# One block's forward transform by tokens mod 4, and wider VectorE instructions, in a fused convolution and feed-forward kernel

## The chip, the cores and the metric

The kernel runs on one core of one Trainium2 chip. A core has a matrix engine (TensorE, PE in the profile), a vector engine (VectorE, DVE), a scalar engine (ScalarE, ACT), a general engine (GpSimd, POOL) and a queue engine (SyncE, SP) that here mostly issues DMA transfers. The metric is the device time of one execution in microseconds (us); three runs of the kernel before took 908.04 to 908.59, median 908.13.

## The reference

Two layers of the same two steps, each added to its input: a gated long convolution (A) and a gated feed-forward network (B). S is 2048 tokens, D is 576, F is 4608. Cut to what matters:

```python
def A(q, k, v):                                # q is the normalised x
    kv = shift4(k, shift_k) * v                # four taps along the tokens
    y  = irfft(rfft(kv, 2*S) * rfft(ssm_k, 2*S))[:S]      # causal long convolution, per column
    return q * (y + kv * ssm_D)
def B(x):
    return (gelu(x @ w_gate) * (x @ w_up)) @ w_down
x = q
for layer in range(2):
    x = x + A(layernorm(x), k, v)
    x = x + B(layernorm(x))
```

## The kernel before, in words

**Blocks and units.** The 2048 tokens are four chunks (blocks) of 512. The convolution depends on neither layer's input, only on k, v and the filter, so its result y is made once for each block and used by both layers. A unit is one chunk of one layer; there are eight. The convolution is done blockwise in the frequency domain. Block m's product k\*v (`kvt`, from the tap products in L254 and L260) is turned into a spectrum `kc`, which has four row groups (`kt` 0 to 3) of 128 frequencies with two planes (`s`, real and imaginary, of 576 columns). The filter's block becomes a spectrum `hh`, later `hr`. VectorE multiplies spectra (`mul`, L337 for the real part as one instruction of 2 x 576 columns, L340 for the imaginary part as two of 576, since there the planes of the second factor are crossed), joins the two products (L343), adds over earlier blocks (L558), forms sums and differences of row groups (`both`, L363), shifts them against the block before (`shifted`, L368) and folds them (`fold`, L593 and L594). TensorE's inverse (L383) makes y of it. Spectra that later blocks need are written to DRAM (`Kd`, `Hd`) by GpSimd and read back as `kr` and `hr`.

**Two ways forward.** `fwd` with `fwd_eo` serves block 1's k\*v: for each pair of row groups, plane and column half, four matmul terms give an even and an odd part, and `cross` (L332) adds and subtracts them straight into `kc`. This is 8 calls of 8 matmuls. Here a pair of row groups of kc is ready after half of the calls. `fwd4` with `quarter` serves the filter and blocks 2 and 3: the tokens are taken mod 4, a call has two terms, `cross` writes partial sums in float32 (`ab`, `cd`), and `second` (L671) adds and subtracts these into all four row groups. This is 8 calls of 4 matmuls, and more VectorE work. In both, a matmul is split into two 64-row halves (`both_steps`, L309); between the two steps stands a placeholder on ScalarE or VectorE (`hold`, L1149) that frees the banks in order.

**Feed-forward.** Each of the eight units is visited three times, a third of the hidden columns each time: 24 phases. A phase has 12 gate/up tiles of 18 matmuls (`gu`, L1120, 216 in all, 64 rows, 512 columns), whose results ScalarE and VectorE turn into `hT` (L1714 to L1724), and then 192 matmuls of 64 rows and 288 columns (`dn`, L1793) whose sums VectorE adds into `x_c` (L1823 to L1831). Unit 0 is visited first; then come the others in pairs.

**Order.** A planner in the kernel writes the order of the instructions out by hand: it keeps a model of the time on TensorE, VectorE and ScalarE (`Pace`; the `C_` constants are its costs) and between two feed-forward tiles puts in convolution work that, by that model, is ready (`fill` with queues `V`, `U`, `Pq`, `aq`, `vq`). A prologue of the first 40 us, ordered by a list scheduler, does block 0's convolution, the filter's first spectra and the normalisation of unit 0.

**Rows.** A unit's normalised rows come in four groups of 128 tokens (`xn`, L1033) and must be turned to columns (`xnT`). `spread` (L1072) does it with two DMA transposes on SP's queue (L1075). `spreads` (L1105) gives a group instead to `turn_row` (L1128), which does it with nine TensorE transposes (L1136) and a copy, if by the planner's time it comes within 5 us (`SLOW`) of the end of the visit.

**Names that the change touches.** `prod`, `mul`, `join`, `both`, `shifted`, `fold`, `second`, `step`, the pools `kcp` (spectra) and `ybp` (sums of row groups), the prologue's products, and one call of `fill` at the start of a visit.

## Time and profile before

| what | value |
| --- | --- |
| median of three runs | 908.13 us |
| the profiled execution | 908.22 us, of which the span is 906.4 |
| TensorE busy in the span | 901.6 us |
| VectorE busy | 556.9 us |
| ScalarE busy | 365.6 us |
| GpSimd busy | 149.1 us |

The span runs from the first to the last instruction of the profiled execution; the time of that run holds 1.8 us more. A row of a group of instructions reads: line, engine, operation, output<-inputs, shape, count, then busy time, mean duration of one in ns, and idle time of the engine before them with what ended it. A row of the chain of waits reads: start, duration, engine, operation, line, count. It is the chain of work that ended last, followed back. "cps" is the convolution's PSUM bank, "ps" the prologue's, "gu" and "dn" those of the feed-forward network.

### The profile page before, as it was taken

The numbers are of one execution on the slowest core, as the hardware profiler recorded it, in microseconds if no ns is written. First come the engines' busy times: TensorE is split into PE (matmuls) and PEld (weight loads), VectorE is DVE, ScalarE is ACT, GpSimd is POOL, SyncE is SP. The second block draws the span as 40 slices with busy tenths as digits, with TensorE's granted clock in tenths as the row PEclk, the third lists the DMA queues.
The fourth block names the chain that finished last, engine by engine and source line by source line (L and its number), as shares of the span: only waits on it lengthen the run. The fifth ranks groups of instructions, "written<-read, shape, count | busy, mean of one in ns | idle before, by whom it ended". The sixth has DMA issues, their size and how long they took to land.

```text
span 906.4 us, 24221 instructions
## 1 busy us (share of the span) xinstructions
PE 901.6 (99%) x10445; PEld 597.4 (66%) x10445; DVE 556.9 (61%) x1127; ACT 365.6 (40%) x677; POOL 149.1 (16%) x311
## 2 busy tenths in 40 slices
PE   9999999999999999999999999999999999999998
PEld 7757656577576575775766756757757657667666
DVE  8899988744899946668899734453333334433332
ACT  7785346634534456455245233351121224321211
POOL 5543104220223012321022002220000002100000
PEclk9999999999999999999999999999999999999999
DMA  9999966976529303995943702852720821887640
GB/s 246 310 246 266 263 161 115 197 233 128 196 67 243 105 2 73 276 186 125 234 162 82 160 18 72 149 107 66 135 80 3 157 79 10 142 182 181 132 105 27
DMA packets 128414, 129.70 MB, mean 143 GB/s; under 512 B 43570, under 2 KB 120627, under 8 KB 128308
## 3 DMA queue, kind: packets, MB, share of 16 engines
q1 hardware_dynamic: 119282, 93.22, 48.4%
q0 software_dynamic: 8880, 34.36, 11.2%
q8 instruction: 81, 1.33, 0.6%
q10 hardware_dynamic: 146, 0.59, 0.2%
q14 instruction: 25, 0.20, 0.1%
HBM read 106.91 MB, written 11.80 MB: 131 GB/s over the span
## 4 chain that ended last, share of the span: by engine, by line
PE 96%; DVE 1%; ACT 1%; POOL 1%; issue 0%; ACTq 0%; DVEq 0%
PE gu L1120 61%; PE dn L1793 29%; PE cps L309 2%; PE ps L283 2%; PE ps L1364 0%; PE ps L1499 0%; PE ps L1120 0%; PE dn L1752 0%; PE dn L1761 0%; PE ps L1275 0%; POOL rstd L1583 0%; ACT junk L958 0%; PE ps L1335 0%; PE cps L383 0%; DVE x_c L1823 0%
## 5 line engine op out<-in xcount | busy, mean ns | idle before, releaser
L1120 PE MATMUL gu<-xnT,wgu 64*128 64x512 bf16 x5148 | 561.2, 376 | 0.2
L1120 PEld LDWEIGHTS <-wgu 64*128 64x128 bf16 x5220 | 292.2, 94 | 262.5 <-issue 1.5
L1793 PE MATMUL dn<-wd,hT 64*128 64x288 bf16 x4512 | 293.7, 283 | 0.0
L1793 PEld LDWEIGHTS <-hT 64*128 64x128 bf16 x4512 | 252.8, 94 | 27.6
L1724 DVE TENSOR_TENSOR hT<-ga,gu 128x512 bf16<-128x512 f32 x174 | 119.4, 686 | 170.8 <-ACT ga L1723 170.6
L1723 ACT ACTIVATE ga<-gu 128x512 f32<-128x512 f32 x174 | 103.8, 597 | 285.5 <-PE gu L1120 285.4
L1714 ACT ACTIVATE ga<-gu 128x512 bf16<-128x512 f32 x112 | 66.9, 597 | 138.3 <-PE gu L1120 133.6
L1716 DVE TENSOR_TENSOR hT<-ga 128x512 bf16<-128x512 bf16 x113 | 47.1, 420 | 51.1 <-ACT ga L1715 50.9
L1715 ACT CAST ga<-gu 128x512 bf16<-128x512 f32 x112 | 64.9, 579 | 0.0
L951 POOL TENSOR_SCALAR means<-s 128x1 f32<-128x1 f32 x28 | 18.4, 661 | 255.4 <-DVE x_c L1823 227.6
L1829 DVE SCALAR_TENSOR_TENSOR x_c<-dn,means,x_c 128x576 f32<-128x576 f32 x28 | 22.8, 815 | 29.6 <-PE dn L1793 29.6
L1831 DVE TENSOR_TENSOR x_c<-x_c,dn 128x576 f32<-128x576 f32 x32 | 24.0, 750 | 26.4 <-PE dn L1793 26.4
L327 ACT ACTIVATE eo<-cps 128x576 f32<-128x576 f32 x40 | 25.9, 651 | 27.5 <-PE cps L309 18.3
L966 POOL TENSOR_TENSOR rstd<-ve,neghalf_t 128x1 f32<-128x1 f32 x56 | 34.9, 624 | 4.7
L343 DVE TENSOR_TENSOR prod<-prod 128x576 bf16<-128x576 bf16 x64 | 29.0, 453 | 1.0
L1810 DVE TENSOR_TENSOR xn<-x_c,dn 128x576 bf16<-128x576 f32 x15 | 11.3, 753 | 25.5 <-PE dn L1793 23.2
L994 ACT ACTIVATE yh<-y,rstd 128x576 f32<-128x576 bf16 x28 | 21.4, 769 | 11.1 <-PE dn L1793 9.8
L671 DVE TENSOR_TENSOR kc<-ab,cd 128x288 bf16<-128x288 f32 x64 | 25.4, 449 | 0.0
L453 POOL DMA_DIRECT2D kr<-Kd x20 | 11.0, 549 | 86.9 <-DVE prod L337 86.9
L958 ACT ACTIVATE junk<-x_c,nm 128x576 bf16<-128x576 f32 x28 | 21.5, 768 | 2.0 <-POOL nm L951 1.6
L951 POOL TENSOR_SCALAR nm<-s 128x1 f32<-128x1 f32 x28 | 8.0, 286 | 79.1 <-DVE x_c L1004 79.0
L332 DVE TENSOR_TENSOR ab<-eo 128x288 f32<-128x288 f32 x40 | 16.1, 451 | 7.5 <-ACT eo L327 7.5
(179 smaller groups left out, 627.9 us busy)
## 6 DMA issues: line engine op xcount, KB each, us to landing
wgu<-in_B_w_gate_dram SPq DMA_DIRECT2D x45, 576.0 KB, 5.6
wd<-in_B_w_down_dram SPq DMA_DIRECT2D x30, 864.0 KB, 6.9
wgu<-in_B_w_up_dram SPq DMA_DIRECT2D x45, 512.0 KB, 7.6
hr<-Hd POOLq DMA_DIRECT2D x32, 288.0 KB, 5.6
kr<-Kd POOLq DMA_DIRECT2D x24, 288.0 KB, 5.5
Kd<-kc POOLq DMA_DIRECT2D x12, 288.0 KB, 6.5
k<-in_A_k_dram POOLq DMA_DIRECT2D x3, 1008.0 KB, 10.0
wgu<-in_B_w_up_dram SPq DMA_DIRECT2D x45, 64.0 KB, 7.2
```

Source lines behind the costliest of these rows:

```text
L327: nc.scalar.activation(out=eo[:], in_=ps[:, :, 0:HW], func=ACT.Copy, scale=scale)
L343: self.nc.vector.tensor_tensor(out=dst, in0=pr[:, 0, :], in1=pr[:, 1, :], op=ALU.subtract if part == 0 else ALU.add)
L671: nc.vector.tensor_tensor(out=into[k][:, plane, cols], in0=a, in1=b, op=op)
L951: nc.gpsimd.tensor_scalar(out=v["nm"][:], in0=v["s"][:], scalar1=-1.0 / D, scalar2=None, op0=ALU.mult)
L966: nc.gpsimd.tensor_tensor(out=v["rstd"][:], in0=ve[:], in1=neghalf_t[:, 0:1], op=ALU.pow)
L1120: nc.tensor.matmul(cols(pair[:, s, :]), lhsT=w[r0:r0 + HK, k, gi * P:(gi + 1) * P], rhs=cols(xnT[r0:r0 + HK, blk_of[k], :]), start=(k == 0 ...
L1714: nc.scalar.activation(out=ga[:, 0, :], in_=pair[:, 0, :], func=ACT.Gelu_apprx_tanh)
L1715: nc.scalar.copy(out=ga[:, 1, :], in_=pair[:, 1, :])
L1716: nc.vector.tensor_tensor(out=hT[:, fi, :], in0=ga[:, 0, :], in1=ga[:, 1, :], op=ALU.mult)
L1723: nc.scalar.activation(out=ga[:], in_=pair[:, 0, :], func=ACT.Gelu_apprx_tanh)
L1724: nc.vector.tensor_tensor(out=hT[:, fi, :], in0=ga[:], in1=pair[:, 1, :], op=ALU.mult)
L1793: nc.tensor.matmul(acc[:, g, 0:HW], lhsT=lhs[r], rhs=wn[r, g * HW:(g + 1) * HW], start=step == 0 and fi == 0, stop=step == 1 and fi == FP - 1)
```

## The change

1. Block 1's k\*v goes forward through `fwd4` like blocks 2 and 3; `fwd` and `fwd_eo` are gone. `kc` of a block is one tile of four row groups instead of four tiles, and is complete for all row groups at the same time. Its four row groups are written to `Kd` together.
2. The imaginary product is one instruction of 2 x 576 columns, which reads the second factor's planes in reverse order. `second` is one instruction of 2 x 288 columns for two row groups, `shifted` one of 2 x 576, and a fold takes two of 2 x 576 where it took four of 576, with reversed planes too. The tiles of `yb` are laid out to allow it (four tiles of 2 x 2 x 576 instead of sixteen of 576).
3. At the first visit, too, the planner may put convolution work (here two tap products) ahead of the first gate's `hT`, up to START = 2.1 us of its own time.
4. The constants of the planner's costs that went with the narrow instructions are dropped.

```diff
@@
-        self.kcp = pool("c_kc", N_KC)
-        self.ybp = pool("c_yb", 4 * RT)
+        self.kcp = pool("c_kc", 1)
+        self.ybp = pool("c_yb", RT)
@@ mul
-            for s in range(2):
-                nc.vector.tensor_tensor(out=pr[:, s, :], in0=K[:, s, :], in1=H[:, 1 - s, :], op=ALU.mult)
+            nc.vector.tensor_tensor(out=pr[:], in0=K[:], in1=H[:, ::-1, :], op=ALU.mult)
@@ shifted
-        self.nc.vector.tensor_tensor(out=prev[:], in0=now[:], in1=prev[:],
+        self.nc.vector.tensor_tensor(out=prev, in0=now, in1=prev,
                                      op=ALU.subtract if part == 0 else ALU.add)
@@ step, shift
-                for sg in range(2):
-                    prev = self.yb[(1 - part, kt, sg)]
-                    self.shifted(nyb[part, kt, sg], prev, part)
-                    z[(part, kt, sg)] = prev
+                prev = self.yb[kt][:, 1 - part, :, :]
+                self.shifted(nyb[kt][:, part, :, :], prev, part)
+                z[kt] = self.yb[kt]
@@ step, fold
-                    w["free"] = self.acp.tile([P, 2, D], BF16, tag="ac", name="w")[:, 0, :]
+                    w["free"] = self.acp.tile([P, 2, D], BF16, tag="ac", name="w")
+                    free = w["free"][:]
+                else:
+                    free = z[1][:, :, 0, :]
+                a, b = z[0][:, ::-1, sg, :], z[1][:, ::1 if sg else -1, sg, :]
+                self.nc.vector.tensor_tensor(out=free, in0=a, in1=b, op=ALU.add)
+                self.nc.vector.tensor_tensor(out=a, in0=a, in1=b, op=ALU.subtract)
                 for plane in range(2):
-                    a, b = z[plane, 0, sg][:], z[plane ^ sg, 1, sg][:]
                     up, down = (sg, sg + 2) if sg == 0 or plane else (sg + 2, sg)
-                    nc.vector.tensor_tensor(out=w["free"], in0=a, in1=b, op=ALU.add)
-                    nc.vector.tensor_tensor(out=a, in0=a, in1=b, op=ALU.subtract)
-                    w[up, plane], w[down, plane], w["free"] = w["free"], a, b
+                    w[up, plane], w[down, plane] = free[:, plane, :], z[0][:, 1 - plane, sg, :]
@@ step, second
-                        a, b = ab[s][:, n, :], ab["cd"][:, n, :]
-                        if n == 0:
-                            outs = ((0, s, ALU.add), (2, s, ALU.subtract))
-                        else:
-                            up = ALU.subtract if s == 0 else ALU.add
-                            outs = ((1, 1 - s, up), (3, 1 - s, ALU.add if s == 0 else ALU.subtract))
-                        for k, plane, op in outs:
-                            nc.vector.tensor_tensor(out=into[k][:, plane, cols], in0=a, in1=b, op=op)
-                        when = t.on_dve(2 * C_BF)
+                        rows = ((slice(0, 8, 7), slice(4, 2, -1)), (slice(1, 3, 1), slice(5, 7, 1)))[s][n]
+                        nc.vector.tensor_tensor(out=into["all"][:, rows, cols], in0=ab[s][:], in1=ab["cd"][:],
+                                                op=ALU.subtract if n else ALU.add)
+                        when = t.on_dve(C_M0)
@@ step, steps
-            if m > 1 or filt:
-                for h in range(2):
-                    for e in range(2):
-                        for s in range(2):
-                            self.Pq.append((limit, 0.25, fwd4(filt, e, s, h)))
-                return
-            for kt in range(2):
-                for s in range(2):
-                    for h in range(2):
-                        self.Pq.append((limit, 0.49, fwd(kt, s, h)))
+            for h in range(2):
+                for e in range(2):
+                    for s in range(2):
+                        self.Pq.append((limit, 0.25, fwd4(filt, e, s, h)))
@@ start of a visit
-            if at:
-                fill(t.pe + C_GU + 1.1, False, conv.left > 0)
+            fill(t.pe + (C_GU + 1.1 if at else START), False, conv.left > 0)
```

More of the change, by code (lines that the diff above doesn't have):

```diff
@@ L567, in run @@
             def run():
-                b = self.both(acc[kt - 2, part][:], acc[kt, part][:])
-                for sg in range(2):
-                    nyb[(part, kt - 2, sg)] = b[sg]
+                if kt - 2 not in nyb:
+                    self.plane_tiles(nyb, kt - 2)
+                self.both(acc[kt - 2, part][:], acc[kt, part][:], [nyb[part, kt - 2, sg] for sg in range(2)])
                 return lambda when: None
@@ L605, in step @@
         for kt in KTS:
-            ends = lambda part: [(now, 2 * C_EVD, both(kt, part)), (now, 2 * C_TB, shift(kt - 2, part))]
+            ends = lambda part: [(now, 2 * C_EVD, both(kt, part)), (now, C_M0, shift(kt - 2, part))]
             if m == 1:
@@ L626, in step @@
         for sg in range(2):
[L627 removed]
+            self.V.append((now, 2 * C_M0, fold(sg)))
         ab = {}
@@ L1470, in product @@
                     def product(m=m, part=part, h=h):
[L1471 to L1473 removed]
+                        if part == 0 and not h:
+                            t_ = conv.ybp.tile([P, 2, D], BF16, tag="yb", name="yb")
+                            for n in range(2):
+                                A[n, m] = t_[:, n, :]
+                        conv.prod(part, kc[m], h0[m], A[part, m], slice(0, D) if h is None else half[h])
                     pA[part, m, h or 0] = step = add("DVE", 1.2 if h is None else 0.75, product, (K0[m] if h is None else [K0[m][h]]) + H0[m])
```

99 lines of the change are left out of this document (28 added, 71 removed).

## The prediction

> **What bounds the kernel now.** I read the page's span and busy rows first, then the clock slices.
>
> ```profile
> span 906.4 us, 24221 instructions
> PE 901.6 (99%) x10445; PEld 597.4 (66%) x10445; DVE 556.9 (61%) x1127; ACT 365.6 (40%) x677; POOL 149.1 (16%) x311
> ```
>
> TensorE idles 4.8 us of 906.4. The busy times by stretch say where, and how close VectorE comes:
>
> ```profile
> core 0: us, PE busy (x) PEld busy (x) DVE busy (x) ACT busy (x) POOL busy (x), PEclk, DMA share, GB/s
> 0.00:40.10 40.10, 38.32 (x351) 30.22 (x353) 35.72 (x87) 29.74 (x50) 22.86 (x49) 1.00 1.01 282
> ...
> 44.56:64.78 20.22, 20.21 (x194) 11.02 (x195) 20.05 (x42) 16.15 (x34) 8.57 (x6) 1.00 0.98 245
> ...
> 80.55:104.87 24.32, 24.32 (x236) 13.08 (x234) 23.80 (x54) 12.92 (x25) 3.83 (x8) 1.00 0.97 317
> ...
> 142.20:155.81 13.61, 13.49 (x218) 10.85 (x215) 12.62 (x33) 8.43 (x17) 6.00 (x13) 1.00 0.52 89
> 155.81:868.41 712.60, 712.58 (x8330) 468.38 (x8331) 404.61 (x795) 260.20 (x486) 98.23 (x216) 1.00 0.56 129
> 868.41:906.40 37.99, 35.21 (x373) 22.43 (x368) 12.33 (x19) 7.17 (x12) 0.00 (x0) 1.00 0.13 40
> ```
>
> The granted clock is 1.00 throughout. TensorE loses 1.78 us in the prologue, 2.78 in the tail, 0.12 before 155.81, and 0.02 in the 712.6 us after that. So past 155.81 any TensorE work removed is time removed, and VectorE, busy 57% there, costs nothing. Before it VectorE is nearly as full as TensorE (20.05 of 20.22, 23.80 of 24.32), and block 1's whole chain on it must be ready by 155.81. The chain of waits shows that the two are level there:
>
> ```profile
> 104.87 11.76 PE dn L1793 x192
> 116.63 13.60 PE gu L1120 x126
> 130.23 1.09 PE cps L383 x8
> 131.31 2.05 PE gu L1120 x18
> ...
> 142.20 0.87 ACT junk L958 x2
> ...
> 154.28 0.81 DVE kc L671 x2
> 155.09 0.69 DVE x_c L1823 x2
> 155.81 23.49 PE gu L1120 x216
> ...
> 191.55 23.31 PE gu L1120 x216
> ```
>
> The release is the last of eight DMA transposes of unit 1's rows, which stand on SP's queue one behind another:
>
> ```profile
> L1075 SPq DMA_TRANSPOSE xnT<-xn x8: 1219/1254/2471, 142.9 to 153.3; - x8
> ...
> DMA to landing us min/median/max: 2.5/2.6/4.3
> ```
>
> The last starts at 153.3 and lands 2.6 us later, at 155.9: just where the next gate/up phase begins (155.81).
>
> **The change part by part.** *1. TensorE, block 1's k\*v.* Eight calls of eight 64-row matmuls (64) become eight of four (32). A 64-row matmul with 288 columns is half of a pair of the down projection's kind: 11.76 / 96 pairs = 0.1225 us (the row at 104.87: 192 matmuls). The 16 pairs removed are 16 x 0.1225 = 1.96 us. They stand amid full TensorE (24.32 busy of 24.32), so they come off the path.
>
> *2. TensorE, one row turned by nine transposes.* The reordering that I took from the two programs adds 18 TensorE rows: row 2 of unit 1's input, so far sent by DMA, goes through `turn_row` 112 matmuls into the phase ahead of 155.81. Its price is bounded by transposes that the trace has:
>
> ```profile
> 7.01 1.39 PE ps L1393 x20
> 9.97 0.45 PE ps L1320 x8
> 39.30 0.62 PE ps L1604 x8
> ```
>
> These are 0.070, 0.056 and 0.078 each, so nine cost 0.50 to 0.70. They run in 128-row form amid 64-row matmuls. What that costs shows around the inverse (above): eight 128-row matmuls take 1.09, against 8 x 0.1225 = 0.98, and the 18 gate/up matmuls behind them 2.05, against 23.31 / 12 = 1.94 (a phase of 216 without interruption, the row at 191.55), so 0.11 going in and 0.11 coming out. I take 0.50 + 0.22 = 0.72 (bounds 0.5 without any cost of the turn, 0.92 with both highest). TensorE's sum is -1.96 + 0.72 = -1.24 us.
>
> *3. VectorE, block 1.* The rows for what is merged and added:
>
> ```profile
> L254 DVE TENSOR_TENSOR kvt<-k,skc 128x1152 bf16<-128x1152 bf16 x24 | 17.9, 751 | 0.1
> L340 DVE TENSOR_TENSOR prod<-kr,hr 128x576 bf16<-128x576 bf16 x40 | 16.1, 449 | 0.0
> L337 DVE TENSOR_TENSOR prod<-kr,hr 128x1152 bf16<-128x1152 bf16 x20 | 14.8, 748 | 0.0
> ...
> 120.06 0.82 DVE L368 TENSOR_TENSOR yb<-yb 128x576 bf16<-128x576 bf16 x2
> 120.79 0.75 DVE L558 TENSOR_TENSOR ac<-hr,prod 128x576 f32<-128x576 bf16 x1
> ...
> 71.44 1.56 DVE L671 TENSOR_TENSOR hh<-ab,cd 128x288 bf16<-128x288 f32 x4
> ...
> 124.33 0.45 DVE L593 TENSOR_TENSOR w<-yb 128x576 bf16<-128x576 bf16 x1
> ...
> 127.98 0.46 DVE L594 TENSOR_TENSOR yb<-yb 128x576 bf16<-128x576 bf16 x1
> ```
>
> Two 576-wide operations issued together occupy about 0.74 (120.06 to 120.79); the 1152-wide one that replaces them shows 0.75 and lets the next start after 0.67. So a merge saves 0.07, a start-up and no throughput. Up to the folds block 1 has eight such products (-0.5) and four shifts (-0.3). The eight folds run from 124.33 to 128.44, 0.49 apart because each waits for the last; four wide ones at about 0.75 take 3.0 (-1.0). The filter's `second` step, four narrow operations in 1.47 (71.44 to 72.91), becomes two wide at 0.67 (-0.5 over its four). Two tap products of 0.67 move ahead of the first gate (-1.4). Against these, the new forward adds a `second` step: eight wide operations of 0.67 (+5.4), on a source in float32, for which L558's 0.75 at 576 wide is the nearest row. The sum is +5.4 - 0.5 - 0.3 - 1.0 - 0.5 - 1.4 = +1.7 us for VectorE ahead of block 1's inverse. In TensorE's order the inverse follows gate/up matmul 162 of the phase instead of 126: two tiles, 3.9 us, later, while the phase itself begins 1.96 earlier, at 114.67. So it would stand at 114.67 + 162 x 0.1079 = 132.15 instead of 130.23: 1.9 later on the clock, as much as its operands are, and it need not wait.
>
> *4. What follows the inverse.* With it the chain inverse, gate, norm and transposes shifts by 1.9 us, while TensorE arrives 1.24 earlier; in before the two met. Three things close this gap. Row 2 no longer stands on SP's queue (two transposes of 1.25 each, -2.5 on the queue). Six pairs of the next block's filter leave this phase for later ones, which takes 6 x 0.1225 = 0.74 from TensorE's side of the meeting (it is paid back later). Against it, SP issues that phase's third weight load ahead of the transposes, so they stand behind its issue; I put that at nothing, since it comes while the norms are still under way, and under (c) price what it could cost. I laid the operations of the new order end to end with the durations above. The inverse's second half ends at 136.4, the gates' and squares' chain gives xn rows at 144.8, 146.2, 147.7 and 149.15, TensorE reaches the nine transposes at 147.2 and waits 0.3 for row 2, and row 3's two DMA transposes land at 153.1 to 155.2. The two-step products with row halves wait for placeholder instructions on ScalarE, which in the new order stand behind squares:
>
> ```profile
> 149.83 0.77 ACT L958 ACTIVATE junk<-x_c,means 128x576 bf16<-128x576 f32 x1
> ```
>
> TensorE would stand behind such a square three times, 0.2 to 0.25 each. Unit 1 then begins at about 154.7 (153.7 to 155.6) instead of 155.81. That is -1.1, plus the 0.74 that comes later: -0.4. So of TensorE's -1.24 about 0.9 us goes into new waits.
>
> *5. Parts at nothing.* The two products ahead of the first gate fill an idle stretch:
>
> ```profile
> 43.82 0.69 DVE L1724 TENSOR_TENSOR hT<-ga,ps 128x512 bf16<-128x512 f32 x1 [2.59 <-ACT ga L1723]
> ```
>
> 1.34 into 2.59; if the kernel's first product slipped instead, at most 0.7 would be lost. The prologue's wide products run beside TensorE's 38.32 of 40.10; its last waits are for sums and roots on ScalarE and GpSimd, not for them (0 to 0.2 either way). The wider operations of blocks 2 and 3 lie under 712.58 of 712.60 TensorE time, VectorE at 57%: nothing. One y copy moves from ScalarE to VectorE; both have room there. Block 1's four `Kd` rows are written together and later on GpSimd's queue; their reader, block 2, works past 155.81, where no wait shows, so 0 (a wait there would appear in that stretch).
>
> Sum: 906.4 - 1.24 + 0.9 = 906.06, rounded 906.1. The profiled execution took 908.22, 1.8 more than its span, and stands 0.09 over the median of 908.13. So the forecast is 906.06 + 1.82 - 0.09 = 907.8 us.
>
> **The rivals.**
>
> *(a) TensorE's sum alone.* The chain keeps up, and no new wait appears: -1.24 and the 0.12 before 155.81, so 906.8. For it: 0.02 us of waits in 712 us show that the planner's order can hide everything. Against it: level chains at 155.81. 0.20.
>
> *(b) The reversed views run VectorE at half rate.* The wide products, and the folds, read one operand with its two halves in reverse order, which no row shows. If that drops it to one element a cycle, the price comes from the float32 rows: 576 wide takes 0.75 against 0.45 in bf16, so 0.3 per 576 and 0.6 per 1152. Twelve such operations ahead of block 1's inverse make +7.2 us; VectorE is otherwise full (23.80 of 24.32), and what idles there (the row below) could hide 58.43 - 56.35 = 2.1. TensorE waits at the inverse and again at 155.81 for about 5 us: 907.8 + 5.1 = 912.9. It decides from the point where the slowdown exceeds some 0.2 us an operation (2.4 in all). For it: float32 operands do lose rate. Against it: the inner run of 576 stays contiguous, and L337's 1152 in two rows runs at full rate. 0.10.
>
> ```profile
> 69.97:128.40 58.43, 58.43 (x708) 39.52 (x705) 56.35 (x125) 23.89 (x45) 9.23 (x17) 1.00 0.94 250
> ```
>
> [...]
>
> *(c) Block 1's chain is later than I laid it.* kc is now complete only after all eight quarters, where before each half freed its own products, and VectorE does 1.7 us more. If the products stall on that, or the third weight load, now ahead of the transposes on SP, holds them by one load's issue, then unit 1 begins at 156.5 to 158.5, not 154.7: 1.8 to 3.8 more, 909.6 to 911.6. Against it: the filter's and block 0's products are there to fill the gap. 0.13.
>
> *(d) The extra turn or its waits cost nothing at this place, while the moved pairs hide in waits:* 906.0 to 906.4. 0.07.
>
> **How the numbers follow.** My forecast has 0.50, with a range of its own of 907.1 to 908.7 (start of unit 1 at 153.7 to 155.6, turn 0.5 to 0.92). The predicted time is 907.8 us. For 8 in 10, the range takes in (a) whole and (d)'s top below, and the lower part of (c) above: 906.3 to 910.0. Below 0.2% (1.8 us, about what a measurement of this kernel tells from no change), that is, under 906.3, lies half of (d) and the edge of (a) and of the bounds: faster 0.11. Above 909.9 lie (b), most of (c) and a little of the bounds of the forecast: slower 0.20. Same: 0.69.
>
> **What would show it.** TensorE's instructions fall by 23 pairs of rows; the L309 group on v and nT is gone; nine transposes from L1136 stand once near 147. In the phase that begins near 114.7, the inverse (L383) starts near 132.2, without idle ahead of it. Unit 1's first gate/up matmul starts near 154.7, with 0.5 to 1.2 us of idle between 142 and there, and after it TensorE is again full. The wide part-1 products show about 0.75; 1.35 means (b). If TensorE waits at the inverse, or unit 1 begins after 155.8, the chain was laid too short; if the idle before unit 1 is under 0.2, (a) was right.

## The result, and the profile after

The changed kernel takes 909.48 us (median of 20 runs, 909.37 to 910.70), the kernel before 908.19 in runs interleaved with them (20 runs, 908.01 to 908.59). The ratio is 1.0015, with a 95% interval of 1.0009 to 1.0022: 1.3 us slower, where 0.3 us faster was forecast. Its first profile is that of its slowest run (910.70). The run `again`, of the same kernel, took 909.38, near the median, and its profile is used here. First its page: span and busy times.

```profile
span 907.6 us, 24074 instructions
PE 900.9 (99%) x10422; PEld 572.6 (63%) x10422; DVE 558.2 (62%) x1032; ACT 366.4 (40%) x678; POOL 144.1 (16%) x311
```

TensorE does 0.7 us less than before (900.9 against 901.6) and idles 1.9 more (907.6 - 900.9 = 6.7, against 4.8). The work came down and waits ate it. The busy times by stretch (columns as in the prediction) say where they are:

```profile
64.78:80.55 15.77, 15.58 (x246) 13.62 (x243) 13.41 (x26) 10.17 (x20) 8.10 (x15) 1.00 1.15 201
80.55:104.87 24.32, 24.32 (x244) 13.69 (x242) 23.11 (x48) 13.44 (x25) 4.82 (x9) 1.00 0.98 273
...
142.20:155.81 13.61, 12.29 (x195) 9.75 (x191) 11.42 (x29) 8.22 (x18) 8.76 (x19) 1.00 0.95 155
155.81:868.41 712.60, 712.06 (x8324) 445.23 (x8322) 406.94 (x732) 261.59 (x488) 96.44 (x214) 1.00 0.55 128
868.41:907.60 39.19, 36.29 (x390) 21.61 (x386) 12.74 (x20) 7.16 (x12) 0.00 (x0) 0.99 0.13 40
```

Most of it is ahead of unit 1: between 142.20 and 155.81 TensorE idles 1.32 us where it idled 0.12. After 155.81 it idles 0.54 where it idled 0.02, around 80 it idles 0.19, and the tail costs 2.90 instead of 2.78. The view of TensorE's waits between 40 and 910 us names them (us in total, times, the longest):

```profile
PE cps L298 <- ACT eo L316: 1.5, 3, 1.1
PE cps L1086 <- DVE xn L983: 0.2, 1, 0.2
PE gu L1070 <- DVE x_c L1780: 0.2, 1, 0.2
```

In the kernel before this view is empty (its 0.12 us ahead of unit 1 has no releaser there). Where the time is gained and lost shows in the starts of the phases. They come from the chain of waits of the changed kernel; the row at 155.53 is TensorE's own timeline, as the chain counts a phase's first matmuls to the one before.

```profile
103.19 11.76 PE dn L1744 x192
114.94 17.48 PE gu L1070 x162
132.43 1.09 PE cps L365 x8
133.51 2.05 PE gu L1070 x18
...
147.71 0.68 PE cps L1086 x9
...
191.88 23.31 PE gu L1070 x216
...
229.54 23.31 PE gu L1070 x216
...
411.62 23.31 PE gu L1070 x216
```

```profile
153.21 0.30 PE L298 MATMUL cps<-ht,T 64*128 64x288 bf16 x2 [1.09 <-ACT eo L316]
...
155.53 2.12 PE L1070 MATMUL gu<-xnT,wgu 64*128 64x512 bf16 x18
```

| start of | before | after | difference |
| --- | --- | --- | --- |
| unit 0's second `dn` phase | 104.87 | 103.19 | -1.68 |
| the gate/up phase with the inverse | 116.63 | 114.94 | -1.69 |
| the inverse | 130.23 | 132.43 | +2.20 |
| unit 1's first gate/up (TensorE's timeline) | 155.81 | 155.53 | -0.28 |
| the next visit | 191.55 | 191.88 | +0.33 |
| the phase after it | 228.73 | 229.54 | +0.81 |
| the phase at 411 | 410.54 | 411.62 | +1.08 |
| end of the span | 906.4 | 907.6 | +1.2 |

Read downwards: 1.68 us are gained by 103; 1.41 of them are gone when unit 1 begins (0.68 for the turn and 1.34 of waits and what else the turn costs, less the 0.61 of the pairs that left); five pairs of filter matmuls that left this phase (TensorE's timeline shows 7 from 139 us on where there were 12) are paid in the next (5 x 0.1225 = 0.61, which is the step from -0.28 to +0.33); and 0.5 more goes in each of two later phases of blocks 2 and 3, of which 0.2 comes back between them.

### The profile page after: what moved, and what is told of

It is laid out like the page before. It is cut to its first block, busy times and chain, and to the rows that moved or that the text cites. A ratio compares the mean times of both kernels' runs of the same rounds, so it can differ in the third digit from the quotient of the medians.

```text
span 908.9 us, 24074 instructions
## 1 busy us (share of the span) xinstructions
PE 901.1 (99%) x10422; PEld 576.0 (63%) x10422; DVE 558.3 (61%) x1032; ACT 366.6 (40%) x678; POOL 143.9 (16%) x311
## 4 chain that ended last, share of the span: by engine, by line
PE 94%; DVE 2%; DMA 1%; ACT 1%; issue 1%; POOL 1%; SPq 0%; ACTq 0%; DVEq 0%
PE gu L1070 61%; PE dn L1744 28%; PE ps L282 2%; PE cps L298 1%; DMA hn<-in_A_ssm_k_dram 1%; DVE kc L625 0%; DVE cd L321 0%; DMA xnT<-xn 0%; PE ps L1314 0%; DVE x_c L1780 0%; PE ps L1451 0%; PE ps L1070 0%; PE dn L1703 0%; PE dn L1712 0%; PE cps L365 0%
## 5 line engine op out<-in xcount | busy, mean ns | idle before, releaser
L1070 PEld LDWEIGHTS <-wgu 64*128 64x128 bf16 x5220 | 282.0, 94 | 273.6 <-issue 2.4
L1744 PEld LDWEIGHTS <-hT 64*128 64x128 bf16 x4512 | 242.8, 94 | 37.6
L901 POOL TENSOR_SCALAR means<-s 128x1 f32<-128x1 f32 x28 | 10.7, 384 | 262.8 <-DVE x_c L1774 224.5
L316 ACT ACTIVATE eo<-cps 128x576 f32<-128x576 f32 x48 | 30.9, 651 | 28.4 <-PE cps L298 21.5
L625 DVE TENSOR_TENSOR kc<-ab,cd 128x576 bf16<-128x576 f32 x40 | 29.2, 753 | 0.5
L321 DVE TENSOR_TENSOR ab<-eo 128x288 f32<-128x288 f32 x48 | 19.4, 453 | 7.5 <-ACT eo L316 7.5
L915 POOL TENSOR_SCALAR ve<-ss 128x1 f32<-128x1 f32 x56 | 16.5, 295 | 45.2 <-ACT junk L908 44.3
```

The source lines that it names most:

```text
L316: nc.scalar.activation(out=eo[:], in_=ps[:, :, 0:HW], func=ACT.Copy, scale=scale)
L625: nc.vector.tensor_tensor(out=into["all"][:, rows, cols], in0=ab[s][:], in1=ab["cd"][:], op=ALU.subtract if n else ALU.add)
L1070: nc.tensor.matmul(cols(pair[:, s, :]), lhsT=w[r0:r0 + HK, k, gi * P:(gi + 1) * P], rhs=cols(xnT[r0:r0 + HK, blk_of[k], :]), start=(k == 0 ...
L1744: nc.tensor.matmul(acc[:, g, 0:HW], lhsT=lhs[r], rhs=wn[r, g * HW:(g + 1) * HW], start=step == 0 and fi == 0, stop=step == 1 and fi == FP - 1)
```

## The experiments

Each was first a guess at the 1.4 us ahead of unit 1 or at the 0.5 behind it. The guesses were, in the order in which they came up: the weight load that now stands ahead of the transposes on SP; ScalarE's order, which holds TensorE 1.09 us at 153.21; three chains that end together, so that taking one away only shows the next; the wide instructions themselves; the planner's smaller costs, which change the order; and block 1's chain as a whole. "Before" below is always the kernel before, measured beside that version: 908.11 to 908.19.

### The same kernel again, and the weight load

`again` is the changed kernel unaltered. `load_late` holds the third weight load back until unit 1's transposes are issued; nothing else in any engine's order changes.

> The changed kernel once more, for its spread and a second profile. Its twenty runs so far fell into groups near 909.4, 909.8 and 910.7, and the profiled one (span 908.9) belongs to the slowest. Theory A (the weight load that now stands ahead of unit 1's DMA transposes on SP's queue makes them late): the groups differ by how the load's packets and the transposes' meet, so a profile of a run near 909.4 (span 907.6) shows TensorE's wait for the last transpose at 157.07 (0.91 us) gone or small, and the rest of the trace the same. Theory B (the loss lies in TensorE's wait for ScalarE, 1.09 us at 152.35, behind a gate): that wait is the one that changes, and the wait for the transposes stays near 0.9.

> The changed kernel with the third weight load of that phase put behind unit 1's transposes on SP's queue, as before; no other engine's order changes. Theory A: the transposes land in 2.6 us instead of 4.2, the last by about 153.5, TensorE starts unit 1 when its own work is done, near 155.8 instead of 157.07, and the time falls by 0.3 to 1.3, to 908.2 to 909.1. Theory B: TensorE arrives at 155.8 whatever the transposes do, ScalarE's wait decides, and the median changes by less than 0.2 (909.3 to 909.6).

```diff
-            if due[0][0] > t.pe + (HOLD if near else SOON):
+            if due[0][0] > t.pe + (HOLD if near else SOON) or due[0][2:] == (load_wgu, 11) and xn_done.get(1, 0) < RT:
                 break
```

`again` took 909.38 (909.36 to 909.76, 11 runs), `load_late` 909.39 (909.36 to 909.41, 11 runs). So the load is not the cause of the loss. It is seen in the slowest run's profile. Here are SP's timeline in that profile (910.70) and the transposes' own rows there, with the time to landing (minimum, median, maximum):

```profile
140.90 0.59 SPq L843 DMA_DIRECT2D wgu<-in_B_w_gate_dram  x1
...
145.29 9.52 SPq L1025 DMA_TRANSPOSE xnT<-xn  x6
```

```profile
L1025 SPq DMA_TRANSPOSE xnT<-xn x6: 1199/1242/2289, 145.3 to 153.3; - x6
...
DMA to landing us min/median/max: 2.6/4.2/5.4
```

and TensorE waits there once more than at the median:

```profile
PE gu L1070 <- DMA xnT<-xn: 0.9, 1, 0.9
```

In `load_late` the landing is back at 2.6:

```profile
L1025 SPq DMA_TRANSPOSE xnT<-xn x6: 1231/1242/2712, 145.1 to 153.1; - x6
...
DMA to landing us min/median/max: 2.5/2.6/4.6
```

The transposes land later while the load is under way (median 4.2 in the slow run, 3.6 in `again`); in `again` TensorE waits for none of them. With the load behind them 11 runs lie within 0.05 us. So in this order the spread comes with the load; the 1.3 us does not. (Later versions, in other orders, spread over 0.3 us and more with the load held back too.) The versions below hold the load back too, except `old_forward`, `cut_after` and `wide_old_plan`.

### The old forward transform, and no turn

`old_forward` gives block 1 the old forward transform back (`fwd` and `fwd_eo` as before) and keeps all else. `late_no_turn` sends row 2 by DMA again (`SLOW` 5.0 to 0.0).

> The changed kernel with block 1's k*v forward as before (eight calls of eight matmuls), everything else as changed. The planner puts its weight load behind the transposes and all eight transposes on SP's queue again, so this is before with wide VectorE instructions and the two early tap products. If the wide instructions cost nothing and the loss comes with the new forward through what the planner makes of it: 907.9 to 908.4, level with before. If the wide instructions themselves cost time (a wait of 0.1 for both inputs of each in the later forwards, reversed planes): 908.7 or more.

> As load_late, and row 2 of unit 1 is again turned by DMA (no nine transposes on TensorE, eight transposes on SP). Theory A with the price of the turn as predicted (0.7 on TensorE): TensorE gains 0.7, but the last transposes are issued 2.5 later and land near 155.9, level with TensorE; the time is 0.2 to 0.7 below load_late. If the transposes on one queue are what bounds unit 1's start even without the load: level with load_late or above it by up to 0.5.

`old_forward` took 912.02 (910.46 to 914.19, 5 runs): slower than either kernel. The profile is that of its fastest run; what the others lose beyond it was not profiled. TensorE's longest waits there are for VectorE's `hT`, and unit 1 begins at 157.78, with no wait just ahead of it:

```profile
PE dn L1785 <- DVE hT L1708: 0.5, 1, 0.5
...
PE gu L1111 <- DVE hT L1716: 0.4, 1, 0.4
```

Undoing one part let the planner make another order, so this run does not price the forward transform alone. That the order makes it slow, and not the old forward transform or the wide instructions, is shown by `wide_old_plan`, further down, which has both.

`late_no_turn` took 916.82 (915.90 to 917.25, 4 runs):

```profile
PE gu L1070 <- DVE kvt L253: 3.6, 1, 3.6
PE gu L1070 <- DMA xnT<-xn: 3.1, 1, 3.1
```

Eight transposes in a row were issued until 155.2 and landed by 160.5; besides, the new order puts four tap products ahead of an eviction. The 3.1 us for DMA alone is more than the turn's 0.68. Behind these waits TensorE also ran slower for a while: its granted clock was 0.50 from 158 to 162 us and 0.67 from 162 to 164, and the 214 gate/up matmuls from 160.53 took 24.63 us, 1.54 over 214 x 0.1079. So part of what this version loses is the clock. The turn costs time on TensorE and is worth more than it costs; it is not where the change loses.

### ScalarE's order ahead of unit 1

TensorE's 1.09 us at 153.21 ends with ScalarE's `eo`. ScalarE's timeline (`again`) shows what stood in front of it:

```profile
150.90 0.63 ACT L316 ACTIVATE eo<-cps 128x576 f32<-128x576 f32 x1
151.84 0.78 ACT L944 ACTIVATE yh<-y,rstd 128x576 f32<-128x576 bf16 x1 [0.32 <-POOL rstd L916]
152.53 0.63 ACT L316 ACTIVATE eo<-cps 128x576 f32<-128x576 f32 x1
```

The next unit's `yh` was put ahead of `eo`, and its `rstd`, made on GpSimd, came 0.32 late. `eo_first` makes the planner count that `rstd` 1.5 us later for this unit, so that `eo` goes first. `eo_turn3` does that and turns row 3 on TensorE too.

```diff
-            return max(conv.y_at.get((c, j), NEVER), g.get("rstd_at", NEVER))
+            return max(conv.y_at.get((c, j), NEVER), g.get("rstd_at", NEVER) + (1.5 if g["ui"] == units.index((1, 0)) else 0.0))
...
         while xn_made and (now or xn_made[0][3] <= t.pe):
+            if xn_made[0][0] == 1 and xn_made[0][1] == 3: break
```

> load_late, and in the stretch 149 to 158 ScalarE evicts the filter's spectrum (eo) before the gates of layer 1 instead of behind them, because the planner now counts these gates' roots as 1.5 us later; TensorE's and SP's orders are unchanged, VectorE's changes by a few neighbours. It takes away TensorE's wait of 1.09 us at 152.1. Theory B (that wait is the loss): TensorE reaches unit 1 at 154.5 instead of 155.5, and the time falls by 0.7 to 1.1, to 908.3 to 908.7. Theory C (two chains end together at 155.5: TensorE with its wait, and behind the same late inverse the last transpose, issued at 153.1 and landing 2.5 later): the wait at 152.1 is gone and one of about 1.0 for the transposes takes its place; the time stays within 0.2, 909.2 to 909.6.

> eo_first, and row 3 of unit 1 is also turned by nine TensorE transposes; SP has four DMA transposes left, the last landing near 151.6. Theory C: with both chains out of the way, TensorE pays 0.7 for the second turn and gains the 1.1, so the time falls by 0.2 to 0.6 against eo_first, to 908.8 to 909.3. Theory B: eo_first has the gain already, and this one loses the turn's price against it, +0.6 to 0.9.

`eo_first` took 909.78 (908.65 to 910.45, 11 runs), no better in the median and spread over 1.8 us. The wait for `eo` is gone, and TensorE waits for the transposes instead:

```profile
154.59 0.40 PE L1070 MATMUL gu<-xnT,wgu 64*128 64x512 bf16 x2
155.29 1.90 PE L1070 MATMUL gu<-xnT,wgu 64*128 64x512 bf16 x16 [0.30 <-DMA xnT<-xn]
```

Of the 0.94 us gained ahead of unit 1 (154.59 for 155.53) 0.48 is lost two matmuls later (155.29 - 154.59 - 2 x 0.1079). The profiled run took 909.02, under its median; what the others lose was not profiled. `eo_turn3` takes the transposes away too: 909.41 (909.29 to 909.85). Unit 1 then begins where the prediction had it:

```profile
154.75 3.83 PE L1071 MATMUL gu<-xnT,wgu 64*128 64x512 bf16 x33
```

But the next visit starts at 191.50, behind a wait for VectorE's eviction, only 0.2 ahead of `again` (191.71 in the same view), and the median is where it was:

```profile
191.50 1.26 PE L1071 MATMUL gu<-xnT,wgu 64*128 64x512 bf16 x10 [0.29 <-DVE x_c L1781]
```

Of the 0.78 us gained at unit 1, 0.29 is this wait and 0.12 a pair of filter matmuls that now comes later. So ScalarE's hold was not the only cause. Behind it stand the DMA transposes; with both out of the way unit 1 starts earlier, at the price of a second turn, and VectorE takes part of it at the next visit.

### The wide instructions

`narrow_second` and `narrow_rest` keep the order and issue the wide instructions as the narrow ones they replaced: the first `second` alone, the second products, shifts and folds.

```diff
-            nc.vector.tensor_tensor(out=pr[:], in0=K[:], in1=H[:, ::-1, :], op=ALU.mult)
+            for s in range(2): nc.vector.tensor_tensor(out=pr[:, s, :], in0=K[:, s, :], in1=H[:, 1 - s, :], op=ALU.mult)
...
-        self.nc.vector.tensor_tensor(out=prev, in0=now, in1=prev,
+        for i in range(2): self.nc.vector.tensor_tensor(out=prev[:, i, :], in0=now[:, i, :], in1=prev[:, i, :],
```

> load_late with the planner's order kept, but each wide instruction of `second` issued as two of 288 columns, first the sums and differences that need only the first of the two `cross` results, as before. Twice 0.37 for one 0.67, so +0.07 each on VectorE; in return the first need not wait for the second `cross` result (0.1). In the forwards of blocks 2 and 3 TensorE waits 0.2 for ScalarE's eviction behind VectorE, at 227 and at 409. If the wide form's longer dependence makes these waits: they shrink, and the time falls by 0.2 to 0.5. If they come from the planner's smaller cost for it (0.67 for 0.74), which puts the work closer together: the waits stay or grow, within 0.2 or up to 0.3 more.

> load_late with the planner's order kept, but the imaginary products, the shifts and the folds issued as narrow instructions as before (no reversed view is left but in `second`). Up to the folds that is 0.6 for the products, 0.3 for the shifts and up to 1.0 for the folds more on VectorE. Rival (b) of the prediction, reversed views at half rate: the time falls clearly, by 2 us or more. Otherwise the folds end 1 to 2 us later, TensorE waits for them at the inverse (its slack there is some 0.8), and the time rises by 0.2 to 1.2.

They took 909.47 (909.45 to 909.81) and 909.72 (909.69 to 909.99): the wide forms are worth 0.1 and 0.3 us, not a loss. The groups by line and shape of `again` show their rate; L326 is the forward view, L328 and L553 read reversed planes:

```profile
L625 DVE TENSOR_TENSOR kc<-ab,cd 128x576 bf16<-128x576 f32 x40 | 29.2, 753 | 0.5
L326 DVE TENSOR_TENSOR prod<-kr,hr 128x1152 bf16<-128x1152 bf16 x20 | 14.8, 751 | 0.0
L328 DVE TENSOR_TENSOR prod<-kr,hr 128x1152 bf16<-128x1152 bf16 x20 | 14.7, 752 | 0.0
...
L553 DVE TENSOR_TENSOR yb<-yb 128x1152 bf16<-128x1152 bf16 x6 | 4.5, 758 | 0.2
```

752 against 751 ns: the reversed view costs nothing.

### The planner's cost of `second`

The 0.5 us lost between 191.88 and 229.54 come with waits. This is TensorE's timeline of `again` there, and ScalarE's:

```profile
224.08 1.65 PE L1744 MATMUL dn<-wd,hT 64*128 64x288 bf16 x24
225.94 0.30 PE L298 MATMUL cps<-v,T 64*128 64x288 bf16 x2 [0.21 <-ACT eo L316]
...
226.67 1.41 PE L1744 MATMUL dn<-wd,hT 64*128 64x288 bf16 x20
228.14 0.30 PE L298 MATMUL cps<-v,T 64*128 64x288 bf16 x2
```

```profile
225.24 0.65 ACT L316 ACTIVATE eo<-cps 128x576 f32<-128x576 f32 x1 [1.46 <-DVE cd L321]
```

The kernel before has 28 and 24 down matmuls in the two gaps where this one has 24 and 20:

```profile
223.75 1.90 PE L1793 MATMUL dn<-wd,hT 64*128 64x288 bf16 x28
...
226.35 1.65 PE L1793 MATMUL dn<-wd,hT 64*128 64x288 bf16 x24
```

From the start of these matmuls to that of the next pair both kernels take the same time (1.87 and 1.47 us there, 1.86 and 1.47 here). So the eight matmuls (8 x 0.0613 = 0.49) are what this phase loses; of this only 0.21 shows as a wait in the timeline. The planner now counts a `second` at 0.67 instead of 0.74, believes VectorE free earlier and calls the next pair of block 2's forward transform (`v`) four matmuls (0.25 us) too soon; the pair waits for `eo`, which waits for VectorE. `second_cost` gives `second` its old planning cost for blocks 2 and 3 and changes no instruction.

```diff
-                        when = t.on_dve(C_M0)
+                        when = t.on_dve(C_M0 if m == 1 else 2 * C_BF)
...
-                    self.U.append((done + LAG, C_M0, second(0)))
-                    self.U.append((done + LAG, C_M0, second(1)))
+                    self.U.append((done + LAG, C_M0 if m == 1 else 2 * C_BF, second(0)))
+                    self.U.append((done + LAG, C_M0 if m == 1 else 2 * C_BF, second(1)))
```

> load_late, with the planner's cost of `second` in the forwards of blocks 2 and 3 put back from 0.67 to 0.74 an instruction; the instructions are the same. The planner then leaves 28 and 24 down-projection matmuls between the quarters there, as before, for 24 and 20, and the third block's inverse goes back to two phases. If the smaller cost made TensorE's waits at 226 and 408 (0.21 each, and what lies around them): both waits vanish, and the time falls by 0.4 to 1.0, to 908.4 to 909.0. If they come from VectorE's wide form or from something else: the waits stay, within 0.2 of 909.39.

It took 909.06 (908.80 to 909.49, 11 runs; ratio to before 1.0010, 1.0001 to 1.0019), 0.33 under `load_late`, a little less than the least that was expected (0.4). Its TensorE timeline at the same place:

```profile
224.08 1.90 PE L1744 MATMUL dn<-wd,hT 64*128 64x288 bf16 x28
225.93 0.30 PE L298 MATMUL cps<-v,T 64*128 64x288 bf16 x2
...
226.67 1.65 PE L1744 MATMUL dn<-wd,hT 64*128 64x288 bf16 x24
228.14 0.30 PE L298 MATMUL cps<-v,T 64*128 64x288 bf16 x2
```

The pairs start at the same times as in `again` (225.93 and 228.14), with eight more down matmuls done between them. The next phase starts at 229.05 instead of 229.54, the one at 411 at 410.65 instead of 411.62. Half of this 0.97 is lost again by 518, where a new wait of 0.33 stands, in block 3's inverse. Against the expectation, that inverse stays in one phase, as in the changed kernel; the kernel before has it in two.

```profile
510.80 0.42 PE L298 MATMUL cps<-yb,V 64*128 64x288 bf16 x4 [0.33 <-DVE x_c L1782]
```

### `second` on GpSimd

To take block 1's extra work off VectorE, `pool_early` issues block 1's eight `second` steps on GpSimd and lets the folds come 1 us earlier in the plan; `pool_early_cost` adds `second_cost`.

```diff
-                        nc.vector.tensor_tensor(out=into["all"][:, rows, cols], in0=ab[s][:], in1=ab["cd"][:],
+                        (nc.vector if m > 1 or filt else nc.gpsimd).tensor_tensor(out=into["all"][:, rows, cols], in0=ab[s][:], in1=ab["cd"][:],
...
-                        mark(("z", sg, part), when + LAG)
+                        mark(("z", sg, part), when + LAG - (1.0 if m == 1 else 0.0))
```

> load_late, with block 1's eight `second` instructions on GpSimd instead of VectorE (the planner counts nothing for them on VectorE and takes the folds as ready 1.0 earlier). The inverse goes one gate/up tile earlier, to matmul 144, and the planner turns all four rows by DMA. Theory D (block 1's work on VectorE, 5.4 us of it `second`, sets when the inverse and with it the rows and transposes of unit 1 come, and so takes what TensorE gains): the inverse starts near 130.5, the last transpose lands near 154, TensorE starts unit 1 near 153.5 to 154.5, and the time falls by 0.7 to 2.0, to 907.4 to 908.7. Rival E (the meeting at unit 1 is set by other things, ScalarE's and GpSimd's chains behind the inverse, or GpSimd is too slow for `second`): no fall, or a rise, 909.2 and more.

> Both edits. If the two causes are separate, their differences from load_late add up to within 0.3. With theory D and the first reading of second_cost: 906.6 to 908.1, below the kernel before.

They took 916.88 (916.36 to 919.57, 4 runs) and 917.07 (916.82 to 919.12, 4 runs). One such step takes GpSimd twice VectorE's time (median 1563 ns, where VectorE's `second` on the filter took 754 in this run; the row has minimum, median, maximum), and TensorE stands 5.4 us:

```profile
L625 POOL TENSOR_TENSOR kc<-ab,cd x8: 1391/1563/1917, 76.4 to 98.2; 128x576 bf16<-128x576 f32 x8
```

```profile
PE gu L1070 <- DVE x_c L1780: 5.4, 1, 5.4
```

Three things add up here. VectorE's next partial sums need the buffer that GpSimd still reads (two of them wait 2.7 and 2.6 us for it), and the eviction stands behind them. Behind this wait the granted clock (third column from the end) was 0.50, and the next 18 gate/up matmuls took 3.63 us (84.72 to 88.35) instead of 1.94:

```profile
86.00:88.00 2.00, 2.00 (x12) 0.84 (x10) 1.54 (x4) 0.00 (x0) 0.54 (x1) 0.50 0.59 160
```

And the new order turns all four rows by DMA, for which TensorE waits another 1.7 us at unit 1's start. The test failed: it put longer waits elsewhere and says nothing of what the extra steps cost at unit 1.

### Unit 1 without block 1's chain

`cut_before` and `cut_after` are the two kernels with unit 1's gate taking block 0's convolution instead of block 1's, from 82 us of the planner's time; everything of block 1 is still computed. `cut_later` does it on `second_cost` from 87 us, so that unit 1's gates stand behind the folds as in the changed kernel.

```diff
-            return max(conv.y_at.get((c, j), NEVER), g.get("rstd_at", NEVER))
+            return max(82.0 if g["ui"] == 1 else conv.y_at.get((c, j), NEVER), g.get("rstd_at", NEVER))
...
-            nc.scalar.activation(out=g["yh"][:], in_=conv.y[c][:, j, :], func=ACT.Identity, scale=g["rstd"][:, 0:1], bias=1.0)
+            nc.scalar.activation(out=g["yh"][:], in_=conv.y[0 if g["ui"] == 1 else c][:, j, :], func=ACT.Identity, scale=g["rstd"][:, 0:1], bias=1.0)
```

> The kernel before, but unit 1's gate takes block 0's convolution result instead of block 1's, from a fixed time on the planner's clock (so it computes something else), which cuts the tie between block 1's inverse and unit 1's rows; its four rows are turned by DMA at about 130 to 145, ten us ahead of need. TensorE's instructions are as before. Theory D: TensorE was level with the chain, so 907.9 to 908.3. Rival E: the same.

> The changed kernel with the same cut; the planner turns all four rows by DMA ahead of need, so there is no turn on TensorE and no meeting at unit 1. Theory D (the tie of unit 1's rows to block 1's late inverse costs the change its gain: the waits near 152, the turn): what is left is TensorE's own sum, 1.96 less for the forward, 0.3 lost again up to 103, and 0.5 to 1.0 lost in the forwards of blocks 2 and 3 through the smaller cost of `second`; the time is 0.7 to 1.6 below cut_before. Rival E (the loss comes from the new forward and the wide instructions themselves, anywhere): it stays 0.5 or more above cut_before.

> second_cost (the changed kernel, load late, the old cost of `second` in blocks 2 and 3), with unit 1's gate on block 0's result as in cut_before and cut_after, but from a later time on the planner's clock, so that VectorE does block 1's folds first and the gates only behind them, one to a tile. It is cut_after without gates in the way of VectorE's backlog; the four rows are turned by DMA, there is no turn on TensorE. Theory D (VectorE's longer chain for block 1, and unit 1's rows behind it, take the gain; TensorE's own sum is right): nothing waits between 103 and 155, TensorE starts unit 1 near 154.0 to 154.6, and the time is 906.7 to 907.7, 0.5 to 1.4 below before and cut_before. Rival E (the new forward or the wide instructions cost TensorE time directly): 908.3 or more.

`cut_before` took 908.14 (908.04 to 908.39), the same as before (908.19): its next visit begins 0.31 us earlier (191.06 for 191.37), of which 0.1 is left at the end of the span. `cut_after` took 909.02 (908.79 to 909.62), with a wait that neither kernel has: unit 1's gates now come amid the folds, ScalarE's `yh` waits 3.60 us for VectorE, and TensorE for ScalarE behind it.

```profile
135.03 2.12 PE L1070 MATMUL gu<-xnT,wgu 64*128 64x512 bf16 x18 [1.53 <-ACT ga L1666]
```

`cut_later` has none of these and took 908.56 (908.36 to 908.77; ratio 1.0004, 0.9995 to 1.0013), 0.5 under `second_cost`. But unit 1 begins no earlier: TensorE arrives 1.17 us ahead and waits for an eviction of VectorE.

```profile
155.75 2.69 PE L1070 MATMUL gu<-xnT,wgu 64*128 64x512 bf16 x22 [1.17 <-DVE x_c L1774]
```

What it gains over `second_cost` (the next visit at 191.46 for 191.70) comes from twelve filter pairs ahead of unit 1 where that has seven. TensorE's work was taken out, and even without block 1's gate in the way another engine is the last to be ready at 155.5 to 155.8.

### The wide instructions with the old plan, and the best version

`wide_old_plan` is the changed kernel with the old forward transform, the planner's old costs (products, shifts, folds, `second`) and no work ahead of the first gate. The orders of TensorE, ScalarE, GpSimd and SP are those of the kernel before; only VectorE's instructions are wider. `cost_turn3` joins `eo_turn3` and `second_cost`.

```diff
-            steps = [(ready(items[n][0]), C_M0, mult(n)) for n in reversed(range(len(items)))]
+            steps = [(ready(items[n][0]), 0.76 if items[n][1] else C_M0, mult(n)) for n in reversed(range(len(items)))]
...
-        self.V.append((now, 2 * C_M0, fold(sg)))
+        self.V.append((now, 4 * 0.46, fold(sg)))
```

> The kernel before with the wide instructions alone: old_forward with the planner's costs of before put back (products, shifts, folds, `second`) and no work ahead of the first gate, which gives before's order on TensorE, ScalarE, GpSimd and SP, and on VectorE the same order with wide instructions in the places of pairs. If the wide forms themselves are harmless (reversed views at full rate, 0.07 saved each, some 0.1 of waiting where one needs both inputs): within 0.2 of before, 907.9 to 908.3, and the 912.0 of old_forward came from the planner's smaller costs. If the wide forms cost TensorE time: 908.5 or more.

> eo_turn3 with the old cost of `second` in blocks 2 and 3 (as in second_cost): the best of the parts tried on the changed kernel. If the parts add up: 909.41 less 0.33, so 908.9 to 909.2, still above before. If unit 1's earlier start (154.75) shows once the later waits are gone: 908.3 to 908.7.

`wide_old_plan` took 908.09 (907.89 to 908.54; ratio 1.0000, 0.9991 to 1.0009): the wide instructions by themselves change nothing that can be measured. It differs from `old_forward` (912.02) in the planner's costs and the work ahead of the first gate; no VectorE instruction has another form. So these two, which only move the order, cost `old_forward` 3.9 us in the median with the same instructions (2.6 between the two profiled runs, 910.46 and 907.90). `cost_turn3` took 908.84 (908.71 to 909.18; ratio 1.0008, 0.9999 to 1.0017), the best version of the changed kernel, still 0.7 over the kernel before. In its profiled run (909.17) the phase at 411 starts at 410.57, level with the kernel before (410.54). What it is behind after that, 0.53 at the phase from 553 (553.31 against 552.78), is lost between 481 and 553, where block 3's inverse and `second_cost`'s new wait lie (0.03 behind at 481). What makes that wait was not tested. The rest of that run's distance is in its tail. No version tried beat the kernel before by more than a measurement tells.

## Why the prediction failed, step by step

**TensorE's gain (right, a little less).** Forecast 1.96 us less by the down phase near 103; measured 1.68. Of the missing 0.28, 0.13 is there when the first down phase begins (64.91 against 64.78) and 0.19 is a wait for VectorE's eviction at 79.45, which no step had (0.04 comes back between them).

**The turn (right).** One turn of nine transposes, 0.68 us at 147.71 after a wait of 0.20; forecast were 0.72 at 147.2 after 0.3.

**VectorE ahead of the inverse (right).** The inverse was forecast at 132.15 without a wait. It stands at 132.43 without a wait; 0.27 of its 0.28 is that of the phase in which it stands (114.94 against 114.67).

**What follows the inverse (the first step that failed: its waits were sized too small).** The rows of xn end within 0.3 us of where they were laid (145.05, 146.50, 147.90, 149.25, from VectorE's timeline), and the last transpose goes out at 152.7. But "TensorE would stand behind such a square three times, 0.2 to 0.25 each" did not hold: it stands there once, 1.09 us, and not behind a square alone but behind a `yh` that itself waits for GpSimd. Unit 1 begins at 155.53, not 154.7. Of this 0.83, 0.27 is TensorE's smaller gain and 0.13 a pair of filter matmuls that stayed (five left, not six). The turn took 0.04 less than forecast. The rest, 0.47, is new waits: 154.7 has 0.87 of them in it (the 0.9 of the sum), and they came to 1.34, of which the idle times show 1.20 (1.32 against 0.12).

The experiments add that the term could not be had by taking that one wait away. With it gone the transposes hold TensorE at the same place (`eo_first`). With these gone too (`eo_turn3`) unit 1 does begin at 154.75, but a second turn is paid for it, and VectorE's eviction takes 0.29 at the next visit. Without block 1's gate ahead of unit 1 (`cut_later`) VectorE's eviction holds unit 1 itself. So the chains end within about 1 us of each other there: 154.59 for TensorE and 155.29 for the transposes (`eo_first`), 155.75 for VectorE (`cut_later`); VectorE had been level with TensorE before. That taking one away shows the next is shown; which of them is to be called the cause is not settled, since no run took all of them away at no cost.

**Later blocks (the second step that failed, and the larger: a term put at nothing).** "The wider operations of blocks 2 and 3 lie under 712.58 of 712.60 TensorE time, VectorE at 57%: nothing." The operations are indeed free, as `narrow_second` and `narrow_rest` show. But their planning costs shrank with them, the order moved, TensorE's idle time there went from 0.02 to 0.54, and the phase starts slipped by 0.75 (from +0.33 to +1.08). Giving one cost back (`second_cost`) removed the two waits there (at 226 and 408 us) and took 0.33 off the median. An engine 57% busy over 712 us is full in the stretches where TensorE asks for its results: from 222 to 228 us VectorE is busy 5.86 of 6.00. Taken as independent, this step's 0.75 and the 0.47 of the waits at unit 1 together make the difference between the span of 907.6 and one of 906.4, that of the kernel before; with either of them alone it would still be slower. The other 0.3 of the forecast gain is what TensorE's gain and the tail fell short.

**The rest.** The moved pairs cost 0.61 (forecast 0.74), the tail 0.12 (forecast nothing). The two products ahead of the first gate cost nothing, as forecast: the gate's `hT` starts at 43.71 (43.82 before). Set against the forecast end of 906.06 these are 0.83 at unit 1, -0.13 for the pairs, 0.48 by 229, another 0.48 by 411 with 0.21 gained between, and 0.12 in the tail: 1.57, to 907.6.

**The rivals.** (a), TensorE's sum alone, fell: idle ahead of unit 1 is 1.32, not under 0.2. (b), reversed views at half rate, fell: 752 ns with the planes reversed, against 751 for the forward view (`again`). (c), a late chain, had the right side and the wrong place: the products did not stall on `kc` and the weight load cost the median nothing, yet unit 1 came later than laid. (d), a turn or pairs that cost nothing, fell: the turn took 0.68 and the pairs were paid in full. The range held the time; the sign did not, because the chain was laid end to end with each engine's next instruction taken as ready, and ahead of unit 1 four engines hand over to one another within 4 us.

## What to carry to other kernels

Where chains of several engines end together, work taken off one of them is not time taken off: price the second and third chain at the meeting before counting the first as gained. In a kernel whose order is written by cost constants, cheaper constants are a change of order of their own, in every phase that they reach; test the instructions with the old plan and the plan with the old instructions, one at a time. A share of busy time over hundreds of us says nothing of a stretch of 2 us in which a pair waits for a buffer.

## What was not expected of the hardware

The DMA transposes of unit 1's rows, one behind another on SP's queue, took 1.23 to 1.25 us each at issue (median), but the longest of each row of six or eight 2.0 to 2.7 us (the maxima above, 2.47 before, 1.97 in `again`). With no weight load issued in the 5 us ahead of them they landed 2.6 us after issue (median) in the kernel before, `load_late` and `eo_first`, 2.9 in `late_no_turn` and 3.2 in `eo_turn3`; with a weight load whose issue on the same queue ended 2.4 us before them, 3.6 (`again`) and 4.2 (the slowest run, up to 5.4). GpSimd needed 1.39 to 1.92 us for an addition of 128x576 from float32 to bf16 that takes VectorE 0.75. After waits of TensorE the granted clock fell to 0.50 in some cases: after 5.4 us in `pool_early`, where 18 gate/up matmuls took 1.94 us again from 88.65, 3.9 us after TensorE resumed, and in `late_no_turn` during two waits of 3.6 and 3.1 us with two matmuls between them. A wait of 1.5 us in `cut_after` left it at 1.00, and one of 1.7 us ahead of unit 1 left it at 1.00 in `pool_early` (214 matmuls from 163.91 in 23.27 us) but was followed by 0.50 (166 to 168 us) in `pool_early_cost`.
